# Two-level Strassen for the second product of a fused attention and MLP kernel, one outer product at a time

## The chip, the core and the metric

The kernel runs on one core of a Trainium2 chip. The metric is the device time of one execution in microseconds (us), given as the median over runs. Before the change it is 918.07 us over 3 runs (916.06 to 918.24).

## What is computed

```python
kv  = einsum('bhsd,bhse->bhde', k, v)          # 8 batches, 8 heads, 576 rows, 64
out = einsum('bhsd,bhde->bhse', q, kv)
out = out / sqrt(mean(out**2, -1) + 1e-6) * g_norm
x   = out.transpose(0, 2, 1, 3).reshape(4608, 512)
h   = x @ w_in                                  # 512 -> 2048
g   = maximum(0.01 * h, h)
return g @ w_out                                # 2048 -> 512
```

All of it is float32. In what follows "h" is the first product with its leaky ReLU, "o" the second product.

## The kernel before, in words

The 4608 rows of x are cut into nine blocks of 512. For a block, the 2048 hidden features are cut into four chunks of 512 (c = 0 to 3, `NC` = 4). Block 0 is computed directly (`first_block`). Block 1 uses one level of Strassen's method (in Winograd's form) for both products: seven products of half-size matrices in place of eight, each of them four matmuls 128x256. From block 2 on h uses two levels: 7 x 7 = 49 matmuls 128x128 for a chunk (`product_h_two`, L930); o stays at one level (`product_o`, L973), except that of its seven products the one numbered 2 is itself done by seven matmuls 128x128 (`Second`, L905), which ride in a free quarter of h's PSUM banks.

Names that recur. `ORDER` = (1, 2, 6, 5, 7, 3, 4) is the order of the seven products at one level. A product that is FRESH (1, 2, 5) opens a PSUM bank, and the others add into a bank, so that Winograd's chain sums partly in PSUM. PSUM has eight banks here: `ha`, `hb`, `hc`, `hd` for h, `oa`, `oc` for o, and two for the attention. Each tag has one buffer: a bank that is written again waits until it has been read out.

One step of `product_h_two` is one outer product number k with its seven inner products: four matmuls go to one bank (`ha` or `hc`) and three to another (`hb` or `hd`). Then the banks are read out to SBUF: for k = 1, 6, 5, 4 by ScalarE (ACT) copies (L951), for k = 2, 7, 3 by VectorE (DVE) adds of PSUM to SBUF (L953). Seven steps make a chunk; after them seven DVE adds combine the quarters to the four parts of g (L959 to L968), four ACT activations apply the leaky ReLU (L832), and four adds on GpSimd (POOL) make the four sums of parts that o needs as left sides (`sums_of`, L839 to L848). The right sides of o are sums of w_out's parts; they were made in block 1, lie in DRAM, and are read back for every chunk (L673). The sums of w_in's parts (`combine`, L702) lie in DRAM too, 448 KB for a step, and are streamed through a ring of five homes (`read`, L737).

The order of the work is written out by hand. `pin` keeps instructions in program order on their engine. In the loop of L1136 each of 28 slots of a block takes one step of h and, lagging two slots, one step of an earlier chunk's o (`go_o`). So TensorE (PE) alternates between 1.6 to 1.8 us of h and 1.7 us of o; what is read out from the one is read while PE works at the other. The attention of the next batch is cut into steps that stand in given slots; its loads are issued on SP's queue between the weight reads. The sums of x for the next block are made at slots 20 to 27 (`sides_x`, L752): four adds on DVE, sixteen on POOL.

Of the kernel before, what the change touches and what calls it, by code (L numbers as in the profile page):

```python
# [23 lines left out]
def kernel(  # L24
# [36 lines left out]
    nc = tc.nc  # L61
# [22 lines left out]
    xpool = ctx.enter_context(tc.tile_pool(name="xpool", bufs=3))  # L84
    gpool = ctx.enter_context(tc.tile_pool(name="gpool", bufs=2))
    opool = ctx.enter_context(tc.tile_pool(name="opool", bufs=2))
# [4 lines left out]
    steady = first_done = in_line = False  # L91
# [6 lines left out]

    NW = U * NE * P
    w1_all = consts.tile([P, 2 * NC * NW], F32, name="w1_all")  # L100
    stage = consts.tile([P, 3 * NW], F32, name="stage")
    pairs = consts.tile([P, 4 * NW], F32, name="pairs")
    g_all = [consts.tile([P, 4 * U * N2], F32, name=f"g_{i}") for i in range(2)]

# [57 lines left out]
    def load_first():  # L162

        early = xpool.tile([P, NE * NT], F32, tag="xT", name="early")
# [25 lines left out]
    def make_ident():  # L190
# [9 lines left out]
    w2_sb = [[consts.tile([P, U, DM], F32, name=f"w2_{h}_{c}") for c in range(NC)]  # L200
             for h in range(2)]

    spare_homes = itertools.cycle(("gs1", "gs2", "gs3", "gs4"))

    def spare(n, name, dtype=F32):

        return gpool.tile([P, n], dtype, tag=next(spare_homes), name=name)
# [97 lines left out]
    def block(i):  # L305
        if i not in xTs:
            xTs[i] = xpool.tile([P, NE, NT], F32, tag="xT", name="xT")
        return xTs[i]
# [48 lines left out]
    def outputs(b, lo, hi, e, sums, kv=None):  # L357


        x, n = x_of(lo, hi), hi - lo  # L360
        tiles = att_tiles("o_ps")
        o_ps = [t[:, :n] for t in tiles]
        o_products(b, lo, hi, e, o_ps)
        if kv is not None:
            kv_beside(b + 1, kv, tiles)
        for l in range(2):
            sq = t2k(n, "sq" if e else f"sum{l}")
            nc.scalar.activation(sq, o_ps[l], func=AF.Square)
            if e == 0:
                sums.append(sq)  # L370
            else:
                in_turn(nc.vector.tensor_add(sums[l], sums[l], sq))
        for l in range(2):
            nc.scalar.activation(x[:, 2 * l + e, :], o_ps[l], func=AF.Copy, scale=g_sb[:, e:e + 1])

    def divide(lo, hi, sums):
# [3 lines left out]
        for l in range(2):  # L380
# [4 lines left out]
            if l:  # L385
                act = nc.scalar.activation(rms, rms, func=AF.Sqrt, scale=1.0 / D, bias=eps_sb)
                if first_done:
                    pin(act)
# [3 lines left out]
        for l in range(2):  # L392
            t = t2k(n, "spread")
            nc.scalar.copy(t.rearrange("p (a i) -> p a i", i=E),
                           rms[:, l, :].unsqueeze(2).to_broadcast([P, n // E, E]))
# [9 lines left out]
    def both_outputs(b, lo, hi, sums, kv=None):  # L405
# [8 lines left out]
        for l in range(2):  # L414
            sq = t2k(2 * n, "sq").rearrange("p (e n) -> p e n", e=2)
            nc.scalar.activation(sq, o_ps[l], func=AF.Square)
            sums.append(t2k(n, f"sum{l}"))
            in_turn(nc.vector.tensor_add(sums[l], sq[:, 0, :], sq[:, 1, :]))
        for l in range(2):
            for e in range(2):  # L420
                nc.scalar.activation(x[:, 2 * l + e, :], o_ps[l][:, e, :], func=AF.Copy,
                                     scale=g_sb[:, e:e + 1])
# [217 lines left out]
    def sides_w1(c):  # L640
# [9 lines left out]
        def more():  # L650
# [6 lines left out]
    w2_dram = [[dram.tile([P, 2, U, N2], F32, name=f"w2_{c}_{i}") for i in range(2)]  # L657
               for c in range(NC)]
    t12, t34 = pair(2, 2, U, N2), pair(3, 2, U, N2)
    writes = []  # L660

    def sides_w2(n):


# [5 lines left out]
        def sums(i):  # L670
            t = (t12, t34)[i]
            if n >= NC:
                pin(nc.sync.dma_start(t, w2_dram[c][i]))  # L673
                return
# [6 lines left out]
            if (n, i) == (NC - 1, 1):  # L681

                writes.append((w2_dram[c][i], t))
            else:
                pin(nc.sync.dma_start(w2_dram[c][i], t))
# [3 lines left out]


    GROUPS = (1, 6, 7, 4), (2, 5, 3)

    INTO = {1: (0, 0), 2: (0, 0), 6: (0, 1), 3: (0, 1), 7: (1, 1), 5: (1, 1), 4: (1, 0)}
# [36 lines left out]
    reads = [(c, k) for _ in range(2, NB) for c in range(NC) for k in ORDER]  # L730
    RING = 5
    n_read = 0

    def w_place(n):
        return view(w1_all, n % RING * NG, 7, P)

    def read(to):  # L737
        nonlocal n_read
        while n_read < min(to, len(reads)):
            c, k = reads[n_read]  # L740
            pin(nc.sync.dma_start(w_place(n_read), w1_dram[c][:, SLOT[k], :, :]))
            n_read += 1
# [3 lines left out]
    xt1 = [work.tile([P, 2, N2], F32, tag="xt1", name="xt1"),  # L746
           view(w1_all, RING * NG + 24 * P, 2, N2)]
    xt24 = [work.tile([P, 2, 2, N2], F32, tag="xt24", name="xt24"),
            view(w1_all, RING * NG + 16 * P, 2, 2, N2)]
    xi = view(stage, 0, 3, 7, P)  # L750

    def sides_x(i):  # L752
# [5 lines left out]
        home = i % 2 if i > 1 else 0  # L758
        t1, t2, t4 = xt1[home], xt24[home][:, 0], xt24[home][:, 1]
        if i == 1:  # L760
            t4 = opool.tile([P, 2, N2], F32, tag="o", name="xt4", bufs=6)
# [11 lines left out]
        for js, y in (((1, 7), upper), ((2, 3), lower),  # L773
                      ((6, 4), xt24[home].rearrange("p t r (v n) -> p t r v n", v=2)),
# [9 lines left out]
        def inner(kind):  # L784
            for y11, y12, y21, y22, t1, t2, t4 in batches:
                if kind == 0:
                    add(nc.gpsimd, t1, y12, y11, True)
                    add(nc.gpsimd, t2, y22, t1, True)
                elif kind == 1:
                    add(nc.gpsimd, y12, y22, y12, True)  # L790
                else:
                    add(nc.gpsimd, t4, y21, t2, True)
# [3 lines left out]
    def strassen(tags, left, right, done, order=ORDER, pieces=None):  # L796

        banks = {}  # L800
        for i in order:

            if i is None:
                yield
                continue
# [4 lines left out]
            if pieces and b == tags[0]:  # L810
                if i == 1:
                    homes = [bank] + [ps_m.tile([P, 2, N2], F32, tag=t, name=f"o_{t}")
                                      for t in ("ha", "hc")]
                    ends = [t.rearrange("p u n -> p (u n)")[:, :cols.stop - cols.start]
                            for t, (_, cols) in zip(homes, pieces)]
                for to, (part, cols) in zip(ends, pieces):
                    for r in range(2):
                        matmul(to, lhsT=left(i, part, r), rhs=right(i, part, r)[:, cols],
                               start=(i == 1 and r == 0), stop=(r == 1), skip_group_check=True)
                done(i, ends)  # L820
                yield
                continue
# [8 lines left out]
    def relu(t, src=None):  # L831
        nc.scalar.activation(t, t if src is None else src, func=AF.Prelu, alpha=SLOPE)  # L832
# [6 lines left out]
    def sums_of(c, to):  # L839

        g11, g21, g22, g12 = g_of(c)
        s1, s2, s3, s4 = (gpool.tile([P, 4, P], F32, tag=f"gs{i}", name=f"gs{i}")
                          for i in range(1, 5))
# [37 lines left out]
    gi = view(pairs, 12 * P, 4, P)  # L881

    def inner_w2(c):
        y = w2_sb[1][c]
        t1, t2, t3, t4 = (w2_sb[0][c][:, u, N2 + s * P:N2 + s * P + P]
                          for u in range(2) for s in range(2))
        y11, y12, y21, y22 = (y[:, u, s * P:s * P + P] for u in range(2) for s in range(2))
        add(nc.gpsimd, t1, y12, y11, True)
        add(nc.gpsimd, t2, y22, t1, True)
        add(nc.gpsimd, t3, y22, y12, True)  # L890
        add(nc.gpsimd, t4, y21, t2, True)

    def inner_g(c, half):

        g = g_of(c)[3]
        a11, a21, a12, a22 = (g[:, n, :] for n in range(4))
        s1, s2, s3, s4 = (gi[:, n, :] for n in range(4))
        if half == 0:
            add(nc.gpsimd, s1, a21, a22)
            add(nc.gpsimd, s2, s1, a11, True)  # L900
        else:
            add(nc.gpsimd, s3, a11, a21, True)
            add(nc.gpsimd, s4, a12, s2, True)

    class Second:  # L905


        def __init__(self, n, o, finish):
            self.n, self.o, self.finish = n, o, finish
            c = n % NC  # L910
            g, y = g_of(c)[3], w2_sb[1][c]
            ts = [w2_sb[0][c][:, u, N2 + s * P:N2 + s * P + P]
                  for u in range(2) for s in range(2)]
            self.left = {1: g[:, 0, :], 2: g[:, 2, :], 4: g[:, 3, :],
                         **{k: gi[:, at, :] for at, k in enumerate((5, 6, 7, 3))}}
            self.right = {1: y[:, 0, :P], 2: y[:, 1, :P], 3: y[:, 1, P:N2],
                          **{k: ts[at] for at, k in enumerate((5, 6, 7, 4))}}

        def product(self, k, bank):
            matmul(bank, lhsT=self.left[k], rhs=self.right[k], start=False, stop=True,  # L920
                   skip_group_check=True)

        def done(self, k, bank):
            v, s = INTO[k]
            to = self.o[:, v, s * P:s * P + P]
            add(nc.vector, to, bank, to)
            if self.n % NC == NC - 1 and k == ORDER[-1]:
                self.finish("11", self.o)

    def product_h_two(i, c, quarters, to, second):  # L930

        n0 = 7 * ((i - 2) * NC + c)

        into = {1: (0, True), 2: (0, False), 6: (1, True), 5: (3, True), 7: (3, False),
                3: (1, False), 4: (2, True)}
        banks = {}
# [318 lines left out]
```

## Time and profile before

| | |
|---|---|
| median of 3 runs | 918.07 us (916.06 to 918.24) |
| span of the profiled execution, first to last instruction | 915.5 us |
| the runs lie above that span by | 0.6 to 2.7 us, the median by 2.6 |
| granted TensorE clock | 1.000 |
| PE busy | 909.1 us, 99% |
| DVE busy | 628.2 us, 69% |
| ACT busy | 327.6 us, 36% |
| POOL busy | 367.0 us, 40% |
| start of the first h product of blocks 2, 3, 4, 5 | 227.9, 326.4, 423.3, 520.2 us |
| DMA | 200.06 MB, mean 219 GB/s |

How to read it. The profile is one execution on the chip. Busy time is given for each engine; matmuls overlap each other in it, so a busy PE says only that there was always a matmul under way, and the cost of a matmul is read from the distance of two starts. A float32 matmul is two instructions. An engine's idle time costs something only where the chain of work that ends last runs through it. Rows name a line of the kernel (L636 is the helper that records most adds), the engine, the operation, the tile written and the tiles read, the shape, the count, the busy time and the mean ns of one.

### The profile page before, as it was taken

Reading aid. Unit: us, or ns where it says so; the run is one execution under the profiler, and the core shown is the slowest. Engines: PE = TensorE matmul, PEld = TensorE weight load, DVE = VectorE, ACT = ScalarE, POOL = GpSimd, SP = SyncE. Lnnn points to the kernel's source line nnn. Section 1 sums busy time; section 2 is a strip of 40 time slices with the busy share of each in tenths; the row PEclk is TensorE's granted clock in tenths of the full one; section 3 lists DMA queues with packets and bytes.
Section 4 is the critical chain, followed back from the end, with each engine's and each line's share of the span. In section 5 each row is a group of like instructions: output and inputs, shape, how many; then the busy total and the mean of one; then the engine's idle time right before and its main releaser. Section 6 shows DMA issues by size and latency. Waiting matters only on the chain.

```text
span 915.5 us, 18030 instructions
## 1 busy us (share of the span) xinstructions
PE 909.1 (99%) x6976; PEld 775.6 (85%) x6976; DVE 628.2 (69%) x1168; ACT 327.6 (36%) x645; POOL 367.0 (40%) x440
## 2 busy tenths in 40 slices
PE   8999999999999999999999999999999999999998
PEld 5444448888998999899999999999999999999997
DVE  5876985587457876587756786678659755755565
ACT  5454533242135233533343324332343333223330
POOL 2000246977633472226321642264226422642222
DMA  9999908895599678877896689658765676667632
GB/s 267 243 243 237 239 35 258 263 304 167 175 360 286 224 213 263 235 233 211 255 261 216 219 250 263 230 179 227 224 184 176 188 221 200 184 187 223 199 107 92
DMA packets 90229, 200.06 MB, mean 219 GB/s; under 512 B 9888, under 2 KB 42272, under 8 KB 90144
## 3 DMA queue, kind: packets, MB, share of 16 engines
q1 hardware_dynamic: 79680, 187.04, 69.5%
q10 hardware_dynamic: 10016, 10.69, 3.4%
q8 instruction: 56, 0.92, 0.4%
q0 software_dynamic: 448, 1.18, 0.3%
q14 instruction: 29, 0.24, 0.1%
HBM read 172.39 MB, written 26.48 MB: 217 GB/s over the span
## 4 chain that ended last, share of the span: by engine, by line
PE 95%; DMA 2%; DVE 1%; POOL 1%; issue 0%; ACT 0%; ACTq 0%; DVEq 0%; POOLq 0%
PE o_a L118 18%; PE o_c L118 18%; PE h_ha L118 11%; PE h_hb L118 11%; PE h_hc L118 8%; PE h_hd L118 8%; PE o_acc L118 6%; PE h_ps L118 6%; PE o_ps L118 3%; PE h_a L118 1%; PE h_c L118 1%; PE kv_ps L118 1%; DMA pairs<-in_v_dram 1%; PE h_b L118 1%; PE h_d L118 1%; DMA w<-pairs 1%
## 5 line engine op out<-in xcount | busy, mean ns | idle before, releaser
L636 POOL TENSOR_TENSOR gs<-g 128x512 f32<-128x512 f32 x64 | 81.7, 1277 | 253.3 <-ACT g L832 253.3
L832 ACT ACTIVATE g<-g 128x512 f32<-128x512 f32 x124 | 78.2, 631 | 130.4 <-DVE g L636 130.4
L951 ACT COPY w_all<-h_ha 128x512 f32<-128x512 f32 x84 | 48.9, 582 | 173.9 <-PE h_ha L118 160.5
L118 PE MATMUL o_a<-pairs,gs 128*128 128x256 f32 x384 | 91.3, 381 | 0.0
L118 PE MATMUL o_c<-pairs,gs 128*128 128x256 f32 x376 | 89.2, 380 | 0.0
L636 DVE TENSOR_TENSOR o<-h_hb,o 128x128 f32<-128x128 f32 x104 | 29.8, 286 | 83.3 <-ACT pairs L951 83.2
L118 PEld LDWEIGHTS o_a<-pairs,gs 128*128 128x128 f32 x384 | 69.8, 190 | 9.2 <-POOL pairs L636 1.2
L636 DVE TENSOR_TENSOR o<-o_c,o 128x512 f32<-128x512 f32 (+1 forms) x91 | 61.1, 672 | 24.1 <-PE o_c L118 23.7
L118 PEld LDWEIGHTS o_c<-pairs,gs 128*128 128x128 f32 x376 | 68.3, 190 | 7.6
L636 DVE TENSOR_TENSOR o<-o_a,o 128x512 f32<-128x512 f32 x75 | 51.2, 682 | 28.2 <-PE o_a L118 28.1
L118 PE MATMUL h_ha<-stage,w_all 128*128 128x128 f32 x448 | 59.6, 276 | 0.0
L118 PEld LDWEIGHTS h_ha<-stage,w_all 128*128 128x128 f32 x448 | 56.6, 192 | 3.0 <-issue 0.7
L118 PE MATMUL h_ps<-xT,w_all 128*128 128x512 f32 (+1 forms) x136 | 58.1, 571 | 0.3 <-DVE w_all L258 0.3
L118 PE MATMUL o_acc<-w,g 128*128 128x512 f32 x128 | 57.7, 594 | 0.0
L636 DVE TENSOR_TENSOR g<-g,pairs 128x512 f32<-128x512 f32 x84 | 55.6, 689 | 1.9
L636 POOL TENSOR_TENSOR pairs<-g 128x128 f32<-128x128 f32 x52 | 23.7, 456 | 77.3 <-PE h_hb L118 48.5
L118 PEld LDWEIGHTS h_ps<-xT,w_all 128*128 128x128 f32 x136 | 25.4, 190 | 29.0 <-issue 26.1
L118 PEld LDWEIGHTS o_acc<-w,g 128*128 128x128 f32 x128 | 24.1, 190 | 30.2 <-issue 29.9
L636 DVE TENSOR_TENSOR w_all<-h_hc,w_all 128x512 f32<-128x512 f32 x56 | 38.3, 684 | 15.9 <-PE h_hc L118 15.6
L636 DVE TENSOR_TENSOR o<-h_hd,o 128x128 f32<-128x128 f32 x78 | 22.0, 283 | 38.2 <-ACT pairs L951 38.1
L118 PE MATMUL h_hb<-stage,w_all 128*128 128x128 f32 x336 | 46.7, 275 | 0.0
L636 POOL TENSOR_TENSOR pairs<-w 128x512 f32<-128x512 f32 x4 | 5.3, 1328 | 98.7 <-ACT cut L245 98.7
(229 smaller groups left out, 2262.4 us busy)
## 6 DMA issues: line engine op xcount, KB each, us to landing
w_all<-w SPq DMA_DIRECT2D x196, 448.0 KB, 4.2
pairs<-w SPq DMA_DIRECT2D x56, 512.0 KB, 4.3
out_dram<-o ACTq DMA_DIRECT2D x35, 256.0 KB, 4.4
v_in<-in_v_dram SPq DMA_DIRECT2D x29, 288.0 KB, 5.5
k_in<-in_k_dram SPq DMA_DIRECT2D x28, 288.0 KB, 5.3
q_in<-in_q_dram SPq DMA_DIRECT2D x56, 144.0 KB, 6.0
q_in<-in_q_dram SPq DMA_DIRECT2D x56, 140.0 KB, 6.0
w<-stage SPq DMA_DIRECT2D x12, 512.0 KB, 4.8
```

What stands on the lines that cost most here:

```text
L118: pin(nc.tensor.matmul(*args, **kw))
L636: ins = eng.tensor_tensor(out_, a, b_, op=ALU.subtract if minus else ALU.add)
L832: nc.scalar.activation(t, t if src is None else src, func=AF.Prelu, alpha=SLOPE)
L951: nc.scalar.copy(q[:, at], bank)
```

## The change

From block 2 on o is done by two levels too, in all seven outer products, and it is no longer interleaved with h chunk by chunk:

- **Order.** The seven outer products j of o run in the order `OUTER` = (1, 6, 7, 4, 2, 5, 3), each over all four chunks at once: 28 matmuls 128x128 (`UNITS`: 16 into bank `oa`, chunk by chunk for the inner products 1, 4, 5, 2, then 12 into `oc` for 7, 6, 3). An item is seven of them. A block's 28 items stand behind the block's h. The last eight of them stand between the seven steps of the next block's chunk 0 (`BESIDE`); chunks 1 to 3 of h run alone.
- **g of the whole block is kept** (`G11`, `G21`, `G12`, `G22`, `GS1`), and its sums are made in place: `outer_g` (the outer sums) and `inner_g` (four sums of quarters for each j, into four tiles `GT` that all j share).
- **Weights.** All sums of w_out's parts, at both levels, lie in DRAM (`fan`, `inner_w2`) and are read in one stream with the sums of w_in, in pieces of up to 448 KB, through five homes (seven after block 3).
- **PSUM is read out** once for each j and bank, 14 times a block, where it was 24 reads 128x512 and 28 reads 128x128. The seven sums that make the output (`o_sums`) run on POOL in the next block's h, at every second slot from 8 on; in the last block on DVE, at the end.
- **g's sums** of a chunk are made in two halves, the first behind step 4, the second behind step 6 (`g_sums`), on DVE with two of seven on POOL; in chunk 3 all on DVE.
- ReLUs, readouts and attention activations on ACT are pinned in program order. x's first-level sums and twelve of the sixteen others go to DVE. The pools' buffers become views of constant tiles.

The core of the diff:

```diff
+    def inner_g(j, k, eng=nc.gpsimd, cs=slice(0, NC)):
+        a11, a12, a22, a21 = (LEFT[j][:, cs, q, :] for q in (Q11, Q21, Q22, Q12))
+        t5, t7, t6, t3 = (t[:, cs] for t in GT)
+        if k == 5:
+            add(eng, t5, a21, a22)
+        elif k == 7:
+            add(eng, t7, a11, a21, True)
+        elif k == 6:
+            add(eng, t6, t5, a11, True)
+        else:
+            add(eng, t3, a12, t6, True)
+    def outer_g(which, c, eng):
+        if which == 5:
+            add(eng, GS1[:, c], G21[:, c], G22[:, c])
+        elif which == 7:
+            add(eng, G21[:, c], G11[:, c], G21[:, c], True)
+        elif which == 6:
+            add(eng, G11[:, c], GS1[:, c], G11[:, c], True)
+        else:
+            add(eng, G11[:, c], G12[:, c], G11[:, c], True)
...
+            for unit, (k, c) in enumerate(UNITS):                    # o_items
+                bank = bank_a if k in KA else bank_c
+                matmul(bank[:, COLUMN[k], :], lhsT=left[k][:, c], rhs=rights[j].at(k, c),
+                       start=first and unit in (0, 16), stop=True, skip_group_check=True)
+                rights[j].gone(unit)
+                if unit == 15:
+                    read_out(oq_a[:, st], bank_a)
+                    if n == 0:
+                        for i in range(NC):
+                            outer_g(6, i, nc.vector)
+                elif unit == 27:
+                    read_out(oq_c[:, st], bank_c[:, :3, :])
+                if n == 2 and unit in (3, 7, 11, 15):
+                    outer_g(3, unit // 4, nc.vector)
+                if after and unit in (15, 19, 23, 27):
+                    inner_g(after, {15: 5, 19: 7, 23: 6, 27: 3}[unit])
+                if unit % 7 == 6:
+                    yield
...
+    def g_sums(c, half, aside):
+        s = slice(half, 4, 2)
+        a1, a6, a7, a4 = (qa[:, s, n, :] for n in range(4))
+        a2, a5, a3 = (qc[:, s, n, :] for n in range(3))
+        g11, g21, g22, g12 = (g[:, c, s, :] for g in (G11, G21, G22, G12))
+        last = [lambda: add(aside, g11, a1, a2), lambda: add(aside, g12, g12, a4)]
+        if aside is nc.vector:
+            last.pop(0)()
+        add(nc.vector, g21, a1, a6)
+        add(nc.vector, g12, g21, a7)
+        add(nc.vector, g22, g12, a5)
+        add(nc.vector, g21, g21, a5)
+        add(nc.vector, g21, g21, a3)
+        for f in last:
+            f()
...
+    def h_block(b, beside, hook):
+        for c in range(NC):
+            last = c == NC - 1
+            steps = h_steps(c, quarters, h_pieces[b][c])
+            for t in range(7):
+                go(steps, 1)
+                if c == 0:
+                    beside(t)
+                if c and t == 1:
+                    g_relu(c - 1, (G21, G22))
+                if c and t == 2:
+                    g_relu(c - 1, (G11, G12))
+                    outer_g(5, c - 1, nc.gpsimd)
+                    outer_g(7, c - 1, nc.gpsimd)
+                if t == 4:
+                    g_sums(c, 0, nc.vector if last else nc.gpsimd)
+                if last and t == 4:
+                    for k in (5, 7, 6, 3):
+                        inner_g(1, k, cs=slice(0, c))
+                if last and t == 5:
+                    g_relu(c, (G11, G21, G22, G12), slice(0, 4, 2))
+                if t == 6:
+                    g_sums(c, 1, nc.vector if last else nc.gpsimd)
+                load_some()
+                hook(7 * c + t)                                       # o_sums on POOL
+        g_relu(c, (G11, G21, G22, G12), slice(1, 4, 2))
+        for k in (5, 7):
+            inner_g(1, k, nc.vector, slice(c, NC))
+        outer_g(5, c, nc.vector)
+        for k in (6, 3):
+            inner_g(1, k, nc.vector, slice(c, NC))
+        outer_g(7, c, nc.gpsimd)
...
+    BESIDE = (2, 1, 1, 1, 1, 1, 1)
```

`h_steps` is the loop of `product_h_two` without the riding product; with each chunk the two bank pairs change places, so that the first step of chunk c + 1 writes the banks that step 5 (k = 3) of chunk c used. In block 1 `fan` adds eight DVE adds, four ACT copies and eight DMA writes for a chunk, and in block 2 twelve POOL adds (`inner_w2`), eight of them each with a DMA write on SP's queue, stand at slots 7 to 18.

## The prediction

> **What bounds the kernel now.** First the head of the page and its groups.
>
> ```profile
> span 915.5 us, 18030 instructions
> PE 909.1 (99%) x6976; PEld 775.6 (85%) x6976; DVE 628.2 (69%) x1168; ACT 327.6 (36%) x645; POOL 367.0 (40%) x440
> ...
> PE   8999999999999999999999999999999999999998
> ...
> L636 POOL TENSOR_TENSOR gs<-g 128x512 f32<-128x512 f32 x64 | 81.7, 1277 | 253.3 <-ACT g L832 253.3
> L832 ACT ACTIVATE g<-g 128x512 f32<-128x512 f32 x124 | 78.2, 631 | 130.4 <-DVE g L636 130.4
> L951 ACT COPY w_all<-h_ha 128x512 f32<-128x512 f32 x84 | 48.9, 582 | 173.9 <-PE h_ha L118 160.5
> ```
>
> PE is full from end to end, and the other engines wait for it or for each other (POOL 253.3 us for the ReLUs). The view of PE's own waits names five groups, 3.2 us in all, all in the first stages. So the time is PE's work plus 3.2 us behind the last matmul (it is through at 912.3 us). What a matmul costs is read from starts, in the timeline of PE inside block 3:
>
> ```profile
> 414.49 0.38 PE L118 MATMUL h_ha<-xT,w_all 128*128 128x128 f32 x2
> ...
> 416.27 1.89 PE L118 MATMUL o_a<-pairs,gs 128*128 128x256 f32 x8
> 418.00 0.38 PE L118 MATMUL h_hc<-xT,w_all 128*128 128x128 f32 x2
> ...
> 419.78 1.06 PE L118 MATMUL h_ha<-stage,w_all 128*128 128x128 f32 x8
> ```
>
> Four matmuls 128x256 take 1.73 us, 0.432 each. The eight 128x128 from 418.00 to 419.78 take 0.223 each (0.2233 over longer stretches, by the starts in nanoseconds).
>
> **The gain on PE.** A chunk's o costs 24 x 0.4323 + 7 x 0.2233 = 11.94 us before and 49 x 0.2233 = 10.94 after: 1.00 us less. 26 chunks give 25.9 us. The last two chunks are 28 products of 128x256 (12.10 us; the very last pays some 0.1 us more for its pieces): 2.4 us. Together **-28.3 us**, if PE stays full. A block then needs 392 x 0.2233 = 87.5 us and the attention's 5 us, 92.7 where two starts lie 96.9 apart.
>
> **Who covers the readouts now.** Before, a step of h was covered by 1.7 us of o. In chunks 1 to 3 h now runs alone, a step of 7 x 0.2233 = 1.563 us, and what DVE, ACT and POOL do between two uses of a bank, or between g and its use, is late by what exceeds the cover. The adds must be looked at with POOL beside them. Block 1, DVE with POOL idle, then both busy (second and third fence):
>
> ```profile
> 144.77 0.41 DVE L636 TENSOR_TENSOR stage<-w_all 128x256 f32<-128x256 f32 x1
> 145.22 0.43 DVE L636 TENSOR_TENSOR stage<-stage,w_all 128x256 f32<-128x256 f32 x1
> 145.56 0.42 DVE L636 TENSOR_TENSOR stage<-w_all 128x256 f32<-128x256 f32 x1
> ```
>
> ```profile
> 159.24 1.38 DVE L636 TENSOR_TENSOR stage<-stage,w_all 128x256 f32<-128x256 f32 x1
> 160.54 1.48 DVE L636 TENSOR_TENSOR stage<-w_all 128x256 f32<-128x256 f32 x1
> 161.95 1.49 DVE L636 TENSOR_TENSOR stage<-w_all,stage 128x256 f32<-128x256 f32 x1
> ```
>
> ```profile
> 158.88 2.87 POOL L636 TENSOR_TENSOR gs<-g 128x512 f32<-128x512 f32 x2
> 161.71 1.44 POOL L636 TENSOR_TENSOR gs<-gs,g 128x512 f32<-128x512 f32 x1
> ```
>
> A 128x256 add of two SBUF tiles takes 0.42 us alone (0.45 to a dependent one, 0.34 to another), and 1.38 to 1.49 us beside POOL's adds, which grow from 1.27 to 1.44: one after the other, a pair in 1.41 us. DVE's adds that read PSUM do not suffer (0.68 us beside POOL or not). Before, DVE's 196 adds to g never met POOL, which waited for the ReLUs. After, POOL has for a block 24 adds 128x512 for `inner_g`, 7 `outer_g`, 7 `o_sums`, 12 halves of g and 8 smaller ones, some 60 us of 92.7, and DVE some 80 adds of two SBUF tiles.
>
> The Trainium skill says why (SBUF — State Buffer, section "Who interferes with whom"): a DVE instruction with two SBUF inputs and a GpSimd instruction that reads SBUF take turns at one shared read port, held for a whole instruction. It speaks against this change, which puts adds of both engines at the same places; by it every meeting costs the later one the rest of the other, as the rows show; without it the two ends below would fall together at the lower.
>
> **Chunk boundaries.** Let T be a chunk's start. Step 4's first bank is full at 4 x 1.563 + 0.89 = 7.15; DVE starts 0.20 later (its idle gap behind PE in the timeline) and adds both banks (0.68 + 0.56) until 8.55. Now five adds of `g_sums` stand in DVE's queue ahead of step 5's readout: 2.1 us alone, until 10.65. Then step 5's first bank is added until 11.33, and the next chunk's first matmul, which writes that bank, could have started at 10.94: **0.4 us** late. With POOL in the way (its two g adds of 0.73 become ready in the same 2 us, and an `o_sums` add of 1.27 stands just ahead) I count three meetings, 0.95 us more: **1.35**. There are two such boundaries in each of seven blocks, and one more in block 2, whose chunk 0 has no o beside its last two steps: 15 x 0.4 to 15 x 1.35. I take 1.0: 15 us.
>
> **From h to o.** In chunk 3 seven adds follow step 4. Free, they end at 11.4; the ReLUs of that half (three left behind the last, 0.42 each) at 12.3, and only then, in ACT's order, step 6's copies (0.58 + 0.48) at 13.4; then DVE's second half until 16.25 and `inner_g(1, 5)` of chunk 3 (0.29). Unit 14 of o needs that. PE gets there at 10.94 + 14 x 0.2233 = 14.07, plus 0.7 for the attention matmuls that stand between: it waits **1.8 us**. With POOL's four adds for `inner_g(1)` (128x384, about 0.98 by the rows of 256 and 512) running from 7.5 to 11.3, three of DVE's seven meet them, and the chain ends 2.2 us later: 4.0 us. Behind it stand on DVE `inner_g`, `outer_g(5)` and the four adds of `outer_g(6)` (0.69 each), then POOL's first add for j = 6 (1.27), which unit 30 needs: another 0.6 to 1.4 us. So 2.4 to 5.4 us a block, seven times; I take 4.0, as the meetings are where both queues are full: 28 us.
>
> **Behind h, inside o.** POOL needs 4 x 1.27 = 5.1 us for a j that lasts 6.25; it keeps up. DVE has, in the nine items from the eleventh on, x's sixteen adds, a tail of the attention and two transposes of 1.24 us: some 17 us of work for 17 us, with up to a dozen meetings. Its read of j = 2's bank may then be late for j = 5. 0 to 2.5 us in the five blocks with attention: 0 to 12 us; I take 4.
>
> **The end.** After the last matmul came one add of 0.29 us and a write; the end came 3.2 us later. Now: the readout (0.2 + 0.56), seven adds 128x512 of 0.69 in a chain, and the write as before (3 us less the add): 8.0 us, **+4.8**.
>
> **Blocks 1 and 2.** `fan` puts eight adds and `inner_w2` twelve where POOL is dense (65.7 us busy of 86.9 in block 1). Below, nothing, if the slack of the interleaved h and o takes them up; above 8 us, as twelve adds of 1.27 us in slots that already hold about 10 us a chunk, with SP's weight reads behind their writes. I take 2.
>
> **The stream.** Pieces of 448 KB are wanted every 1.56 us, 293 GB/s, before loads and stores. The windows show 327 GB/s over 30 us with no wait of PE, and pieces issued five or seven steps (7.8 or 10.9 us) ahead, where a landing takes a median 4.2 us; I cost it at 0, with 10 us as the other end, if one attention load in each block stands in the way.
>
> **Sum.** 918.07 - 28.3 + 15 + 28 + 4 + 4.8 + 2 = **943.6 us**. It is made on the profiled execution's span (915.5 gives 941.0 for the span), and the median stands 2.6 above that.
>
> **Rivals.**
> - *PE stays nearly full* (faster). Place: the hand-over from h to o. If POOL reaches its adds when DVE is through with its own, each stands where the other's gap is; the chain then costs 1.2 us a block and the boundaries 0.2: -28.3 + 15 x 0.2 + 7 x 1.2 + 4.8 = -12.1, 906.0 us. For it: POOL idles between chunks. It decides below 3.4 us of new waits a block ((28.3 - 4.8) / 7). Chance 0.31.
> - *The free chain alone*: -28.3 + 6 + 17 + 4.8 = -0.5, 917.6 us: no change. Chance 0.06: it needs both places to come out at their free length, and nothing else.
> - *The stream or DVE's backlog binds too*: every upper end together is -28.3 + 20 + 38 + 12 + 4.8 + 8 + 10 = +64.5, 982 us. For it: the h stage wants in one stretch what was spread over both. Chance 0.12 for more than 965.
> - The forecast, 921 to 965 us: 0.51.
>
> Range: 903 to 970. Its lower end leaves out the lower third of the faster case, its upper end the worst of the last. A change under 0.3% (2.8 us) can't be told from none here. Faster 0.31, same 0.06, slower 0.63.
>
> **What the profile after would show.** Right: PE's groups of o at 0.223 us from start to start; PE's waits no longer 3.2 us but 50 to 60, at o matmuls released by DVE and POOL (unit 14 and 30) and at h's first bank released by DVE; DVE's adds of 128x256 with a mean well above 0.42. Wrong: those adds at 0.42, or PE's waits under 25 us in all; or most waits ended by DMA.

## The result, and the profile after

The changed kernel takes 1052.6 us (median of 4 runs, 1048.8 to 1055.8) where the kernel before takes 917.3: a ratio of 1.148 (95% interval 1.1445 to 1.1508). The profiled execution is the fastest of the four, 1048.8 us with a span of 1047.1. Slower, as forecast, but by 135 us instead of 26.

The head of the page:

```profile
span 1047.1 us, 20851 instructions
PE 922.0 (88%) x7980; PEld 812.1 (78%) x7980; DVE 725.6 (69%) x1192; ACT 343.8 (33%) x717; POOL 588.9 (56%) x519
...
PE   8999989897977968988997899797989799889896
...
PEclk9999999999999989999999989998999899999998
```

PE is no longer full. POOL's busy time has grown from 367 to 589 us, DVE's from 628 to 726. The row of the granted clock, 1.000 before, has five eights among its nines; its mean is 0.964. PE's waits, by what ended them:

```profile
PE o_a L125 <- DVE stage L645: 41.0, 8, 9.0
PE o_a L125 <- DVE w_all L645: 20.1, 6, 3.8
...
PE o_a L125 <- POOL w_all L645: 8.1, 5, 2.4
```

The columns are total us, count and the longest. Of the first row's eight waits two, 7.8 us, lie in block 1. The other six, 33.2 us, lie at a place that the forecast priced at 4 us: the first matmul of j = 5 writes the bank that j = 2 filled, and waits until DVE has added it to `stage`. Block 2 has the longest. PE's timeline there, then DVE's, then POOL's:

```profile
378.50 1.22 PE L125 MATMUL o_a<-w_all,pairs 128*128 128x128 f32 x4 [8.98 <-DVE stage L645]
...
379.94 1.49 PE L125 MATMUL o_a<-w_all,pairs 128*128 128x128 f32 x6
381.22 0.63 PE L125 MATMUL o_a<-w_all 128*128 128x128 f32 x2
...
384.51 0.39 PE L125 MATMUL h_hc<-xT,w_all 128*128 128x128 f32 x2
384.74 0.39 PE L125 MATMUL h_hc<-xt,w_all 128*128 128x128 f32 x2
```

```profile
359.47 1.76 DVE L645 TENSOR_TENSOR xt<-xT 128x512 f32<-128x512 f32 x1
361.26 1.64 DVE L645 TENSOR_TENSOR xt<-xT,xt 128x512 f32<-128x512 f32 x1
362.83 1.75 DVE L645 TENSOR_TENSOR xT<-xT 128x512 f32<-128x512 f32 x1
364.50 1.75 DVE L645 TENSOR_TENSOR xt<-xT,xt 128x512 f32<-128x512 f32 x1
...
377.81 0.63 DVE L645 TENSOR_TENSOR stage<-o_a,stage 128x512 f32<-128x512 f32 x1
```

```profile
358.95 3.41 POOL L645 TENSOR_TENSOR w_all<-gs 128x512 f32<-128x512 f32 x2 [1.22 <-PE o_a L125]
362.32 1.71 POOL L645 TENSOR_TENSOR w_all<-w_all,gs 128x512 f32<-128x512 f32 x1
364.11 1.60 POOL L645 TENSOR_TENSOR pairs<-gs,w_all 128x512 f32<-128x512 f32 x1
```

From 359 to 366 us four adds of x on DVE and four of `inner_g` on POOL take 1.7 us each, one after the other, where alone they take 0.69 and 1.27. DVE is behind from there on, and the readout at 377.81 stands behind it all. From o's third product to the first matmul of j = 5, 14 to 16 of DVE's 18 to 23 adds of two SBUF tiles in a block (2 to 7) take longer than alone, by 11 to 14 us in sum. The PE rows show a second thing: from 379.94 to 381.22 three products take 1.28 us, 0.427 each, while from 384.51 on they take 0.223. The view by stretches has the granted clock (columns: length, busy time of PE, weight loads, DVE, ACT, POOL, then PE's clock, DMA share, GB/s):

```profile
369.30:378.40 9.10, 0.22 (x2) 0.03 (x1) 9.00 (x15) 0.78 (x3) 6.80 (x7) 0.77 0.00 0
378.60:384.30 5.70, 5.70 (x27) 5.70 (x28) 3.49 (x6) 0.90 (x3) 0.00 (x0) 0.50 0.81 219
384.50:388.00 3.50, 3.50 (x32) 3.41 (x31) 2.32 (x4) 0.00 (x0) 1.44 (x2) 1.00 1.03 287
```

After the wait PE works 5.7 us at half of its clock. Two more of PE's waits, at the first matmul of a chunk of block 7's h, and at unit 14 of its o:

```profile
862.51 0.49 PE L125 MATMUL h_ha<-xT 128*128 128x128 f32 x2 [1.06 <-DVE w_all L645]
...
892.94 0.80 PE L125 MATMUL o_a<-w_all 128*128 128x128 f32 x2 [3.83 <-DVE w_all L645]
```

The units of a block's o are its 196 matmuls 128x128, counted from 0, 28 for each of the seven j: unit 14 is the first that needs a sum of `inner_g` for chunk 3, unit 30 the first that needs one for j = 6, unit 112 is the first of j = 2 and unit 140 the first of j = 5. The whole account is made from the distances between matmul starts. A wait is an excess of over 0.6 us over the clean distance, some 0.16 us more than the idle time in the brackets of a row; half clock is the excess of h's and o's matmuls that began while 0.5 was granted.

| from span 915.5 to 1047.1 us | forecast | measured |
|---|---|---|
| matmuls at their clean distances | -28.3 | -28.3 |
| chunk boundaries (blocks 3 to 8) | +15 | +13.2 |
| h to o, units 14 and 30 | +28 | +30.5 |
| j = 2's readout late, units 140 and 112 | +4 | +36.8 |
| blocks 1 and 2, waits up to o | +2 | +28.1 |
| half clock | none | +27.9 |
| behind the last matmul | +4.8 | +6.9 |
| other waits (8 us) and differences too small to be waits | 0 | +16.5 |

### The profile page after: what moved, and what is told of

Same layout as the page of the kernel before. It is cut to its first block, busy times and chain, and to the rows that moved or that the text cites. A ratio compares the mean times of both kernels' runs of the same rounds, so it can differ in the third digit from the quotient of the medians.

```text
span 1047.1 us, 20851 instructions
## 1 busy us (share of the span) xinstructions
PE 922.0 (88%) x7980; PEld 812.1 (78%) x7980; DVE 725.6 (69%) x1192; ACT 343.8 (33%) x717; POOL 588.9 (56%) x519
## 3 DMA queue, kind: packets, MB, share of 16 engines
q8 instruction: 63, 1.03, 0.4%
## 4 chain that ended last, share of the span: by engine, by line
PE 51%; DVE 28%; DMA 8%; issue 5%; POOL 3%; ACT 3%; SPq 1%; ACTq 0%; DVEq 0%; POOLq 0%
PE o_a L125 13%; PE o_c L125 9%; DVE g L645 6%; PE h_hc L125 5%; DVE stage L645 5%; PE h_ps L125 5%; PE h_ha L125 5%; PE o_acc L125 5%; DVE xt L645 3%; DVE gs L645 3%; PE h_hd L125 3%; PE h_hb L125 3%; DVE xT L645 3%; DMA w_all<-w 3%; DMA q_in<-in_q_dram 2%
## 5 line engine op out<-in xcount | busy, mean ns | idle before, releaser
L645 POOL TENSOR_TENSOR w_all<-g 128x512 f32<-128x512 f32 (+1 forms) x56 | 69.4, 1260 | 73.9 <-PE o_a L125 52.2
L815 ACT ACTIVATE g<-g 128x512 f32<-128x512 f32 (+1 forms) x82 | 45.8, 559 | 104.2 <-DVE g L645 104.2
L645 POOL TENSOR_TENSOR g<-g,g 128x512 f32<-128x512 f32 x28 | 35.6, 1273 | 64.6 <-DVE pairs L645 54.6
L125 PE MATMUL o_a<-w_all 128*128 128x128 f32 x266 | 56.3, 295 | 16.8 <-DVE w_all L645 13.5
L125 PE MATMUL o_c<-w_all 128*128 128x128 f32 x498 | 69.4, 287 | 0.0
L645 DVE TENSOR_TENSOR g<-g,pairs 128x256 f32<-128x256 f32 x112 | 64.3, 574 | 1.9
L125 PEld LDWEIGHTS o_c<-w_all 128*128 128x128 f32 x498 | 64.6, 203 | 0.1
L125 PEld LDWEIGHTS o_a<-w_all 128*128 128x128 f32 x266 | 43.5, 206 | 20.3 <-DVE w_all L645 14.7
L125 PE MATMUL o_a<-w_all,g 128*128 128x128 f32 x354 | 56.7, 278 | 2.5 <-DMA w_all<-w 2.5
L645 POOL TENSOR_TENSOR stage<-stage 128x512 f32<-128x512 f32 x42 | 58.9, 1403 | 0.0
L125 PE MATMUL o_a<-w_all,pairs 128*128 128x128 f32 x140 | 28.0, 346 | 33.2 <-DVE stage L645 33.2
L645 POOL TENSOR_TENSOR w_all<-gs 128x512 f32<-128x512 f32 x28 | 41.9, 1518 | 20.4 <-PE o_a L125 17.9
```

The lines of the kernel that those rows point to most:

```text
L125: pin(nc.tensor.matmul(*args, **kw))
L645: ins = eng.tensor_tensor(out_, a, b_, op=ALU.subtract if minus else ALU.add)
L815: act(nc.scalar.activation(t, t if src is None else src, func=AF.Prelu, alpha=SLOPE))
```

## The experiments

All are edits of the changed kernel (1052.6 us), timed beside the kernel before (916 to 918). Theory A: DVE's adds of two SBUF tiles are late because POOL's adds stand beside them. Theory B: DVE's queue is too long whatever POOL does. Theory C: the half clock is a cost of its own. Theory Q: in blocks 1 and 2 instructions wait in order behind others that wait.

### POOL's adds inside o

Left out (e2), made on DVE instead (e3), left out with POOL memsets of the same tiles in their place (e8), and, the other way round, x's adds put back on POOL (e11).

```diff
e2  - if after and unit in (15, 19, 23, 27):
    + if after and unit in (15, 19, 23, 27) and rights is rights_2:    # block 2 only
e3  - inner_g(after, {15: 5, 19: 7, 23: 6, 27: 3}[unit])
    + inner_g(after, {15: 5, 19: 7, 23: 6, 27: 3}[unit], nc.vector)
e8  + pin(nc.gpsimd.memset(GT[{15: 0, 19: 1, 23: 2, 27: 3}[unit]], 0.5))   # for inner_g
e11 - itertools.chain(sums, inner(0, nc.vector), inner(1, nc.vector), inner(2))
    + itertools.chain(sums, inner(0), inner(1), inner(2))
```

> Edit: from block 3 on the four inner_g adds for each of j = 6, 7, 4, 2, 5, 3 are left out of the computation (the tiles GT keep what inner_g(1) put there); all else stands. POOL is then idle for most of o, while DVE has the same instructions in the same order. Theory A (DVE's adds meet POOL's): DVE's adds of x fall from 1.75 to about 0.7 us, the wait at the first matmul of j = 5 (2.2 to 6.5 us a block) goes away in blocks 3 to 7 and takes some 8 us of half clock with it, and so do the waits at the second inner product of j = 6 (9 us): 1052.6 - 23 - 8 - 9 = about 1012 us (1003 to 1022). Theory B (DVE has too many instructions ahead of j = 2's readout, whatever POOL does): the wait for j = 5 stays at 4 us or more a block, only the 9 us go: about 1043 us.

**1002.6 us** (997.3 to 1004.0), ratio 1.092 (1.089 to 1.095). A's forecast, half a us below its range; B is out. The wait for j = 5 is gone in blocks 3 to 7 and stays at 8.8 us in block 2, where POOL's adds stayed.

> Edit: the 24 inner_g adds of a block for j = 6 to 3 run on DVE instead of POOL; everything is computed. DVE gets 24 x 0.69 = 16.6 us more work a block. Theory A (a pair of adds on DVE and POOL costs 1.75 us, both on DVE cost 2 x 0.69 = 1.38): the time falls although DVE has more to do, because x's adds are back at 0.69; the wait for j = 5 shrinks to under 2 us: 1015 to 1030 us. Theory B (number of instructions in DVE's queue): 16.6 us more work a block on the engine that is late, most of it in o: the wait for j = 5 grows by 3 to 8 us a block, 1075 to 1110 us.

**1011.0 us** (1008.3 to 1014.1), ratio 1.101 (1.099 to 1.104), everything computed. DVE has 168 more adds and the kernel is 42 us faster, 4 us more than A's range allowed. The wait for j = 5 is at most 1.4 us in a block. The same stretch of block 2 on DVE:

```profile
359.09 0.69 DVE L645 TENSOR_TENSOR pairs<-gs,w_all 128x512 f32<-128x512 f32 x1
359.70 0.68 DVE L645 TENSOR_TENSOR xt<-xT 128x512 f32<-128x512 f32 x1
360.42 0.69 DVE L645 TENSOR_TENSOR xt<-xT,xt 128x512 f32<-128x512 f32 x1
```

An add of x and one of `inner_g` take 1.37 us on one engine and 1.7 on two. Of the 34 adds from o's third product to j = 5 in this block 3 are longer than alone, by 1.4 us in sum, where the changed kernel has 14 of 23 and 12.3 us.

> Edit: each of the 24 inner_g adds of a block for j = 6 to 3 is replaced by a POOL memset of the same tile; the sums are left out of the computation, but every wait between POOL and PE on these tiles stays, and POOL still writes SBUF at the same places. Theory A (what hurts is that both engines read SBUF): DVE's adds of x are at about 0.7 us and the time is that of the kernel without these adds, 1002.6, within 8 us. Rival (POOL's being in the chain, or any use of SBUF by it): the wait for j = 5 stays at 4 us or more, 1035 to 1052 us.

**993.5 us** (990.8 to 993.6), ratio 1.083 (1.081 to 1.085), 1 us below A's range. POOL keeps its place in every chain and writes the same bytes, in 0.53 us instead of 1.27. A memset and two DVE adds, then the first of these adds in the changed kernel, beside POOL's add:

```profile
563.63 0.53 POOL L1054 MEMSET w_all<- 128x512 f32 x1 [5.51 <-PE o_a L125]
```

```profile
563.90 1.03 DVE L381 TENSOR_TENSOR sum<-sum,sq 128x384 f32<-128x384 f32 x2 [0.43 <-ACT sq L377]
```

```profile
589.41 1.62 DVE L381 TENSOR_TENSOR sum<-sum,sq 128x384 f32<-128x384 f32 x1
```

The two adds, the first begun inside the memset, take 1.03 us, as the same two do in e2 with POOL idle; in the changed kernel one alone took 1.62. After 350 us, 47 of DVE's adds 128x512 of two SBUF tiles overlap a memset by 0.1 us or more and take 0.63 to 0.69 us; in the changed kernel the 42 that overlap an add of POOL take 1.75 in the median, and 55 adds 128x512 that read PSUM beside an add of POOL 0.68 to 0.69. So it is not POOL's being busy, nor its writing: its reads of SBUF are what meets DVE's adds of two SBUF tiles. (It is 9 us below e2; block 2's wait of 8.8 us is gone too.)

> Edit: x's twelve second-level adds of a block that were moved to DVE are put back on POOL; everything is computed. Theory A (the wait for j = 5 is DVE's backlog of x's adds, each paired with one of POOL's): in the stretch DVE is left with four of x's adds 128x512, the readout of j = 2 is in time, the wait for j = 5 falls from 2.2 to 9.1 us to under 1.5 us: 35 us less waiting and some 10 of half clock; against it POOL gets 12 x 0.73 = 8.8 us in a stretch that it fills to 81% (5.1 of 6.25 us a j), so inner_g for j = 5 and 3 may be 0 to 4 us late in seven blocks: 1008 to 1030 us. Rival (the number of pairs is what counts, not on which engine x's adds stand): POOL's queue grows as DVE's shrinks, its inner_g is late by what DVE was, 1045 to 1060 us.

**1053.0 us** (1051.7 to 1055.8), ratio 1.149 (1.147 to 1.151): the rival's time, and a miss of theory A. The waits' view, then POOL's rows in block 4:

```profile
PE o_a L125 <- POOL w_all L645: 42.9, 18, 4.7
...
PE o_a L125 <- DVE stage L645: 7.5, 2, 4.4
```

```profile
590.42 2.50 POOL L645 TENSOR_TENSOR w_all<-gs 128x512 f32<-128x512 f32 x2
...
603.46 2.48 POOL L645 TENSOR_TENSOR w_all<-pairs 128x512 f32<-128x512 f32 x2
```

Only block 1's two waits, 7.5 us, still end with DVE; those for POOL grow from 8.1 to 42.9. But the rival's reason isn't shown by it. POOL's adds 128x512 here take what they take alone, one behind the other from 590 to 608 us with x's adds between them. From o's third product to its end in block 4 POOL's 37 adds take 39.3 us, and would take some 35.6 alone (by 1.27, 0.73 and 0.46 us for the three sizes). So the wait is mostly POOL's own queue: it has no room for x's twelve adds. What the meetings cost is shown by e2, e3 and e8.

### The hand-over, and everything of POOL

```diff
e7     for k in (5, 7, 6, 3):
    +      if b == 2:
               inner_g(1, k, cs=slice(0, c))       # from block 3 on left out
e12 + if quiet and eng is nc.gpsimd:               # in add(); quiet from block 3's h on
    +     return
```

> Edit: from block 3 on POOL's four adds 128x384 of inner_g(1) in chunk 3 are left out of the computation. POOL is then idle while DVE makes chunk 3's sums of g. Theory A (three of DVE's adds meet POOL's at the hand-over, 2.2 us on the chain): the wait at unit 14 of o falls from 3.2 to 4.0 us to 1.5 to 2.1 us in six blocks, 12 us, with some 5 us of half clock: 1034 to 1041 us. Rival (the chain of readouts, ReLUs and sums is that long without POOL): the wait stays at 3 us or more, 1048 to 1054 us.

**1043.7 us** (1042.4 to 1049.6), ratio 1.139 (1.136 to 1.143), 3 to 10 us above the forecast. The waits at unit 14 fall as A has it, in blocks 7 and 8 from 4.0 to 2.1 us, in sum over six blocks from 21.6 to 10.4. But unit 30 then waits 13.7 us instead of 8.9, for POOL: two fifths of the gain are given back one step later.

> Edit: from block 3's h on every add on POOL is left out of the computation (inner_g, outer_g, o_sums, POOL's two adds of g_sums, the last of x's); DVE, ACT, PE and all transfers keep their instructions and their order. Theory A (what is late in blocks 3 to 8 is DVE beside POOL): no DVE add of two SBUF tiles is above 0.45 us for 128x256 or 0.75 us for 128x512; the boundaries wait 0.4 us each instead of 1.22, unit 14 waits about 1.8 us instead of 3.2 to 4.0, units 30, 112 and 140 wait for nothing but block 2's: 1052.6 - 9 (boundaries) - 10 (unit 14) - 9 (unit 30) - 28 (unit 112 and 140) - 18 (half clock behind them) = about 978 us (970 to 986). Rival (DVE's own order is too long even alone): boundaries above 1 us, unit 14 above 3 us, 1000 us or more. What is left above 917 is then blocks 1 and 2, the end and the free chain itself.

**977.5 us** (972.4 to 984.7), ratio 1.068 (1.061 to 1.074): the forecast. In blocks 3 to 8 DVE's adds of two SBUF tiles are at 0.41 to 0.43 us (128x256) and 0.63 to 0.69 (128x512), units 30, 112 and 140 wait for nothing, unit 14 waits 2.1 us in blocks 7 and 8 (1.3 to 1.8 in blocks 3 to 6, behind the attention's matmuls), and the boundaries wait 0.4 us, once 0.7, for DVE. Of PE's idle times of over 0.6 us, 53 us in sum, 36 now lie in blocks 1 and 2.

### The chunk boundaries

The first edit puts the sums of a chunk's first half behind the next readout; the second leaves POOL's two adds of `g_sums` out.

```diff
e1  - if t == 4:
    + if t == (4 if last else 5):
          g_sums(c, 0, nc.vector if last else nc.gpsimd)
e10   for f in last:
    +     if aside is nc.vector or g_block == 2:
              f()
```

> Edit: in chunks 0 to 2 the first five adds of g_sums on DVE stand behind step 5's readout instead of ahead of it; chunk 3 is unchanged. Theory (order on DVE decides at the boundaries): the waits of 1.22 us at the first matmul of a new chunk, about a dozen of them in the changed kernel's trace, go away, no granted clock changes since none of these waits was followed by a lower clock; 1052.6 - 13 = about 1039 us (1034 to 1044). Rival (the readouts themselves are late, by POOL or by ACT): the boundary waits shrink to 0.8 to 1.0 us and the time stays within 3 us of 1052.

**1053.0 us** (1051.5 to 1056.7), ratio 1.149 (1.147 to 1.151). The theory falls, and so does its rival. The waits of 1.22 us did go; in their place step 3 of the next chunk waits 1.6 and 1.4 us, since its bank is read out behind the displaced sums. Order alone buys nothing where the sums of both halves follow each other.

> Edit: from block 3 on the two of seven adds of g_sums that POOL makes in chunks 0 to 2 are left out of the computation; the five on DVE stay where they are. Theory A (the boundary's 1.22 us is 0.4 us of DVE's order and 0.8 us of two meetings with just these two adds): the wait at the first matmul of a chunk falls to about 0.4 us, 11 waits by 0.83 = 9 us: 1041 to 1046 us. Rival (the five adds are too many at that place by themselves, or the adds of o_sums take the place of the missing ones): the waits stay above 1 us, 1049 to 1055 us.

**1065.6 us** (1063.2 to 1072.8), ratio 1.164 (1.159 to 1.169): work is taken away and the kernel is 13 us slower. Adds of `g_sums` at a boundary of block 7 on DVE, in the changed kernel and then in this one:

```profile
859.36 0.83 DVE L645 TENSOR_TENSOR gs<-g,w_all 128x256 f32<-128x256 f32 x1
...
860.57 1.28 DVE L645 TENSOR_TENSOR g<-g,pairs 128x256 f32<-128x256 f32 x2
```

```profile
867.56 1.37 DVE L645 TENSOR_TENSOR gs<-g,w_all 128x256 f32<-128x256 f32 x1
868.97 1.38 DVE L645 TENSOR_TENSOR gs<-gs,pairs 128x256 f32<-128x256 f32 x1
```

Alone (in e12) the first of these takes 0.42 us, the second 0.42, the two together named x2 0.88. POOL's two short adds of 0.73 us cost DVE 0.41 each. Without them `o_sums`, three adds 128x512 in a row that had stood behind them in POOL's order, reach the boundary and cost 0.96 each at two places. POOL's row there, and PE's:

```profile
865.82 4.24 POOL L645 TENSOR_TENSOR stage<-stage 128x512 f32<-128x512 f32 x3
```

```profile
871.80 0.49 PE L125 MATMUL h_ha<-xT 128*128 128x128 f32 x2 [2.14 <-DVE w_all L645]
```

The wait becomes 2.31 us from start to start. With neither (e12) the waits for DVE there are 0.4 us, once 0.7: so 1.22 is some 0.4 of DVE's own order and twice 0.41 of meetings, and what stands behind a removed instruction counts as much as what is removed.

### The half clock

```diff
e4  + if j == 5:
    +     idle = ps_m.tile([P, 4, P], F32, tag="hc", name="idle")
    +     for _ in range(24):
    +         matmul(idle[:, 0, :], lhsT=ident, rhs=ident, start=True, stop=True)
```

> Edit: 24 additional matmuls 128x128 (24 x 0.2233 = 5.36 us, into a bank that nobody reads) stand in PE's order ahead of the first matmul of j = 5, in all seven blocks: 37.5 us of added PE work. They fill a wait of PE that is there anyway in blocks 2, 4, 5, 6 (9.1, 6.3, 6.5, 6.4 us) and most of 3 and 8 (2.2 and, block 7, 3.6). Theory C (half of the granted clock after a long wait is a cost of its own, some 28 us in all, about 11 of them behind this wait): block 8 adds 5.4, blocks 3 and 7 add 3.2 and 1.8, and the half clock behind blocks 2, 4, 5, 6 goes: about +10 - 11, within 5 us of 1052, with the granted clock between 0.97 and 0.98. Rival (the lower clock is only how the wait is shown, it costs nothing by itself): 1052.6 + 10 = 1063 us or more. If the wait for j = 5 isn't a wait for DVE but scales with PE's own order: 1090 us.

**1054.7 us** (1049.0 to 1056.9), ratio 1.149 (1.146 to 1.153), granted clock 0.974: C. PE does 37.5 us more, and the time is as it was. Block 4's wait, in this kernel and what follows it:

```profile
602.50:609.50 7.00, 7.00 (x64) 6.92 (x63) 6.93 (x9) 0.31 (x1) 5.83 (x5) 1.00 0.01 2
609.50:616.00 6.50, 5.68 (x51) 5.57 (x50) 6.41 (x13) 1.79 (x4) 0.30 (x1) 1.00 0.83 257
```

The clock stays at 1.00, where the changed kernel had 0.87 in the wait and 0.50 for 5 us behind it. Half clock is 19.5 us in this profile, 27.9 without the filling.

### Blocks 1 and 2

```diff
e5    sums(i): ...; - fan(c, i)
    + # in product_o:  if i == 4: fan(n + 1, 0);   elif i == 6 and n: fan(n, 1)
e6  - pin(nc.sync.dma_start(w2_dram[j][:, at * P:(at + 4) * P],
    + pin(nc.gpsimd.dma_start(w2_dram[j][:, at * P:(at + 4) * P],
```

> Edit: in block 1 the call of fan (four DVE adds, two ACT copies, four writes for each half) stands three steps of o later in the program, behind o's readouts of those steps, instead of directly behind the POOL adds whose result it reads; everything is computed. Theory Q (fan's first add waits on DVE for POOL, 8.6 and 4.6 us in the changed kernel's trace, and the readouts of o behind it in DVE's order are late): the waits of 3.4 and 4.8 us at o's matmuls in block 1 go away with 1.7 us of half clock: 1052.6 - 10 = about 1043 us (1040 to 1046). Rival (meetings on the port make the adds of fan themselves too long): the adds only change their place, 1050 to 1056 us.

**1046.7 us** (1041.6 to 1049.4), ratio 1.141 (1.137 to 1.144): 6 us, a little short of Q's range. One of the two waits, 4.8 us, is gone. The other has grown from 3.4 to 4.4 us: fan's first add still waits 8.6 us on DVE for POOL, whose order is behind by more than three steps of o.

> Edit: in block 2 the eight writes of inner_w2's sums are issued on POOL's queue, right behind the adds that make them, instead of on SP's; everything is computed. Theory Q (the writes wait on SP for POOL's adds, up to 4.7 us, and the weight reads stand behind them in SP's order): PE's waits for weight pieces in block 2 (11.6 us in seven waits) go away with 3 to 5 us of half clock: 1037 to 1043 us. Rival (the pieces are late because the transfers share the DMA engines, or because their homes come free late): the waits for weights stay, 1049 to 1056 us.

**1047.1 us** (1043.7 to 1051.2), ratio 1.142 (1.138 to 1.146): between the two forecasts. PE's waits for weights fall from 12.2 to 6.4 us over the kernel, but at two chunk starts of block 2 the waits for DVE grow from 3.4 and 0.5 to 4.3 and 3.5 us. Its runs and those of the changed kernel overlap: a small gain at most, and Q is only half shown here.

### All together

```diff
e9  inner_g for j = 6 to 3 on DVE (e3); fan three steps of o later than in e5; writes as in e6;
    - if last and t == 5: g_relu(c, (G11, G21, G22, G12), slice(0, 4, 2))
    + if last and t == 6: ...
    - if last and t == 4: for k in (5, 7, 6, 3): inner_g(1, k, cs=slice(0, c))
    + if c and t == 3:    for k in (5, 7, 6, 3): inner_g(1, k, cs=slice(c - 1, c))   # b > 2
```

> Five edits together, everything is computed: the 24 inner_g adds for j = 6 to 3 on DVE; fan behind the third and sixth step of the next chunk's o; the writes of inner_w2 on POOL's queue; the ReLUs of chunk 3's first half behind step 6's copies on ACT; from block 3 on POOL's inner_g(1) chunk by chunk, one chunk after its g, so that none of it is left beside chunk 3's sums. Theory (the causes add up): 1011 for the first alone, less 9 for fan (both waits and their half clock), 5 for the writes, 15 for the hand-over (unit 14's wait from 3.2 to 4.0 us down to 1.0 to 1.6, with 5 us of half clock): about 982 us (974 to 992), still slower than before, since some 15 us of boundaries, 7 at the end and the rest of the hand-over are untouched. Rival (one wait only makes room for another, since DVE is the bound from chunk 1 to the end of j = 6): 1000 to 1011 us.

**999.5 us** (996.3 to 1003.2), ratio 1.090 (1.087 to 1.093): half a us below the rival's range. The hand-over behaves (unit 14 from 4.0 to 2.3 us), but the adds put at step 3 of each chunk now reach the boundaries, which wait 2.4 and 1.6 us instead of 1.22. It is the best version that computes everything, and slower than before. With no POOL add at all from block 3 on (e12) the time is still 60 us above the kernel before, so no rearrangement of those adds alone wins.

## Why the prediction was wrong

The direction was right, and so was the main mechanism, DVE's and POOL's adds that take turns; the first three terms were near in size, and three others were not. PE's idle times of over 0.6 us came to 110 us, where 50 to 60 were expected.

- **Gain on PE, -28.3.** Right: -28.3 by the clean distances (2348 more instructions 128x128 by 0.1117, 1344 fewer 128x256 by 0.2162).
- **Chunk boundaries, 0.4 to 1.35 each.** Right: 1.22, and the two ends are what e12 and the rows above show. It is two meetings, not three.
- **From h to o, 4.0 a block.** Right: 30.5 us against 28, all of it in blocks 3 to 8. Unit 14 alone 2.1 without POOL's four adds (1.8 in the forecast) and 4.0 with them, in blocks 7 and 8; unit 30 another 0.9 to 2.6 in five blocks.
- **"Behind h, inside o", 0 to 2.5 us in five blocks, 4 in all.** This step failed. It measured 36.8 us, in six blocks, up to 9.1 in one. The step counted DVE's work free (17 us for 17 us) and named a dozen meetings, but did not multiply: by its own pair cycle a meeting costs about 1 us, so a dozen are 12 us a block, not 2.5. The trace has 14 to 16 lengthened adds in a block, 11 to 14 us. And it asked which engine keeps up, POOL's 5.1 us in 6.25, when the two together must.
- **Blocks 1 and 2, 0 to 8, taken as 2.** Failed: 28.1 us of waits. The step priced the added adds and "SP's weight reads behind their writes", not the wait on another engine that each add or write brings into an in-order queue: 8.6 us of DVE behind POOL in front of o's readouts. e5 shows this for one wait; for block 2's h the share of SP's order, of meetings and of loads stays open.
- **The half clock.** A cost that the sum put at nothing: 27.9 us. The trace of before, with a granted clock of 1.000 and 3.2 us of waits, could not show it; each long wait of PE was priced at its length.
- **The end, +4.8.** +6.9: the seven adds took 4.92 as forecast, the write behind them 1.8 us more than before. The sum's own terms (0.76, seven times 0.69, and 2.7 for the write, less 3.2) make 5.1, not 4.8.
- **The stream, 0 to 10, taken as 0.** PE waits 12.2 us for weights, 10.1 of it in block 2 (part of the rows above).

The rivals: "PE stays nearly full" needed POOL's adds to fall into DVE's gaps, and they do not. "Every upper end" stopped at 982, because its ends for the readouts in o and for the first blocks were too low and it had no half clock. "The free chain" of 917.6 can be estimated from e12: 977.5 less the 36 us that PE idles in blocks 1 and 2, where before it had no idle time of over 0.6 us, and less the 11 us of half clock there, is some 930, 13 above it, in a kernel whose runs spread over 12 us.

## What to carry to other kernels

Where two engines share what reads their operands, add up the work of both as if it were one engine's, and price each meeting (here 0.4 us for a DVE add beside a POOL add of 0.73, about 1 us beside one of 1.27) before asking which engine is behind: an add on the free-looking engine can cost more than one on the busy engine. An add that is moved or removed also lets forward what stood behind it. A wait of PE of over 1.5 us may cost a stretch of half clock beyond its length (up to 1.7 us lost in the shortest stretch of 3.4). Matmuls that only fill the wait cost next to nothing (e4: 2 us for 37.5 us of work), but as placed here they gained nothing either.

## What the runs show of the hardware

- **When the clock falls.** The granted clock falls to 0.5 in pieces of 3.41, 6.83 or 10.24 us, during a wait of PE or up to 3.4 us behind it (the last piece, behind the last matmul, apart). Over the thirteen traces after the change:

| PE idle for | waits | with a fall of the clock |
|---|---|---|
| 0.6 to 1.5 us | 285 | 0 |
| 1.5 to 2.5 us | 110 | 32 |
| 2.5 to 3.5 us | 90 | 68 |
| over 3.5 us | 76 | 76 |

  The Trainium skill (TensorE: Matmul & The Clock Gate, "Part 1: The HAM clock gate") gives a half rate after an idle window of about 3.4 us and says that the window is free-running. The length of the pieces agrees with it, and so does every wait above 3.5 us; but 100 waits of 1.5 to 3.5 us were followed by a fall as well, so a wait shorter than the window is not safe.
- **Writes of POOL do not meet DVE's adds.** Beside the 168 memsets of 0.53 us that stand in place of 168 adds, DVE's adds take 0.42 and 0.69 us, as alone. That fits the turns at a shared read port of which the prediction spoke.
- **Two engines slower than one.** A 128x512 add on DVE and one on POOL take 1.7 us together, two on DVE 1.37.
